# Weight remainders by engine, and two float64 weight chunks brought into the attention: a fused attention, expert and dense kernel

## The chip, the core and the metric

The kernel runs as one program on one core of a Trainium2 chip. The metric is the device time of one execution in microseconds (us), from the first to the last instruction with what the launch adds around it. The core has five instruction queues that matter here: PE (TensorE, matmuls), DVE (VectorE), ACT (ScalarE), POOL (GpSimd) and SP (SyncE, which here only issues DMAs). Each engine works its own queue strictly in order; semaphores tie the queues together.

## The reference

```python
scores = scale * q @ k.T                       # 2 batches, 8 heads, 768 positions, 64 wide
scores = where(is_sink | in_window, scores, -1e9)   # 4 sinks, window of 128
x = softmax(scores) @ v                        # 1536 tokens x 512

logits = x @ w_gate                            # 8 experts, capacity 192 each
order = argsort(-logits.flatten())             # greedy assignment, best pair first
for e in range(8):
    out[mask_e] = maximum(x[mask_e] @ w1[e], 0) @ w2[e]     # 512 -> 1024 -> 512

h = out @ w_in                                 # float64 weights, 512 -> 2048
y = (h * sigmoid(h)) @ w_out                   # float64 weights, 2048 -> 512
```

w1 and w2 come as float32; w_in and w_out come as float64 and reach the chip as pairs of 32-bit words.

## The kernel before

The program has four stages. **Attention** (`attention_band`, about 0 to 109 us) walks 96 heads (12 query blocks of 8 heads, index `n`), as a software pipeline written out by hand: in round `n` TensorE computes the scores of heads `n` and `n+1` (even `n`, `s_mm`), VectorE merges the two key blocks (`s_merge`, L261) and takes the row maximum (`s_max`, L268), ScalarE takes the exponential, TensorE transposes the head `n-5` and multiplies the head `n-13` with the values (`pv`). GpSimd cuts the transposed weights to the band (L299, L302). A dictionary `hooks` runs extra steps in given rounds. Every eight rounds SP gets the loads of a later block (keys three blocks ahead, values two), and TensorE computes the gate's products of one block (`vw`, L370). Scores, gate products and sink products share four PSUM buffers named `s`. **Routing** (to about 138 us) finds the assignment by iterations that go back and forth between VectorE and TensorE. **Experts** (`experts`, 145.5 to 310.4 us) and **dense** (`dense`, 310.4 us to the end) are TensorE loops over weights.

`Weights` feeds these two loops. The weights are 40 chunks of 128 x 2048: 32 of the experts (`k` = 0 to 31, float32), then 8 dense ones (`k` = 32 to 39, float64, "wide"). Each chunk is used as a high part and a remainder, in two halves: `hi` is a ScalarE copy of a half to fp32r (L884), and `lo` is the subtraction raw minus high (L888). A wide half must first be unpacked from 64-bit words into float32 by ten VectorE steps, five for each of its two quarters (`s0` to `s4`, L846 to L862). Raw pieces come through seven buffers `raw`: the step that uses one up issues the next load on SP. Four chunks `wr` are held at a time; `done(k)` lets chunk `k+4` begin. The steps `hi` and `lo` of a coming chunk stand in a list `todo`, those of unpacking in `back`; `pump(items, ops)` is called at fixed places of the TensorE loops (in `evac` after each half chunk of the experts, after each group of `dense`) and takes `items` of the first and `ops` of the second, so it decides where these steps stand in the queues of ScalarE, VectorE and GpSimd. Per expert `e` the TensorE order is `m1(e+1,0)`, `m2(e,0)`, `m1(e+1,1)`, `m2(e,1)`, one chunk each. After each half chunk `evac` takes the result out of PSUM by a ScalarE copy (L1010), a VectorE addition (L1011), a ScalarE step (L1013) and a VectorE subtraction (L1015 or L1017). GpSimd also gathers the experts' rows of `x` by indirect DMA (L956), three at a time.

Before the change a remainder runs on GpSimd, with one exception: while the experts run, every eighth half (`LO_DVE`) runs on VectorE. All sixteen wide remainders run on GpSimd. The unpacking of chunk 32 begins in the last two experts (`W.ahead(4 * E)` and the `ops` of 2 and 3 that `m1`, `m2` and `evac` hand on), with 5 steps per group in the first two groups of `dense`.

## Time and profile before

| | |
|---|---|
| median of 3 runs | 590.63 us (589.99 to 618.26) |
| the profiled execution | 593.17 us |
| its span, first to last instruction | 591.5 us |
| TensorE busy | 552.3 us (93%) |
| VectorE busy | 345.0 us (58%) |
| ScalarE busy | 254.2 us (43%) |
| GpSimd busy | 240.1 us (41%) |
| mean granted TensorE clock | 0.957 |

The shares are averages over four stages with different limits, so they say little by themselves. The views that help are the page's slices (one digit for each 14.8 us), the waits of TensorE, and the instructions in order of time around each wait. Matmuls are pipelined: what counts is the distance from one start to the next, not the length of one.

### The profile page before, as it was taken

What the parts mean: (1) busy time and instruction counts of PE and PEld (TensorE: products, weight loads), DVE (VectorE), ACT (ScalarE), POOL (GpSimd) and SP (SyncE); (2) the same over time, 40 slices, a digit from 0 to 9 for tenths busy, and PEclk for the clock granted to TensorE, in tenths of its full rate; (3) what the DMA queues carried; (4) which work ended last, traced back from release to release, by engine and by line L of the source; (5) the groups of instructions that cost most, each with busy time, mean ns of one, the idle gap of its engine ahead of it and who ended that gap; (6) DMA issues with size and microseconds to landing.
All of it is one profiled execution on the core that took longest, in us unless ns stands there. A gap on an engine that the chain in (4) does not pass through costs nothing.

```text
span 591.5 us, 9262 instructions
## 1 busy us (share of the span) xinstructions
PE 552.3 (93%) x3367; PEld 493.1 (83%) x3369; DVE 345.0 (58%) x852; ACT 254.2 (43%) x488; POOL 240.1 (41%) x212
## 2 busy tenths in 40 slices
PE   8999999547999999899987999999999999999996
PEld 4788788425899898899986888899889988999884
DVE  3665867871356658554787988659436963131312
ACT  4544544451575773776434334362223332222220
POOL 3333333376489799889831331122101230000124
PEclk9999999756999999799988999999999999999999
DMA  7846554053366566666642343233101000000022
GB/s 207 294 144 227 178 187 174 37 213 118 101 214 230 198 235 228 214 217 242 213 147 93 121 142 109 70 107 104 40 1 35 1 1 0 2 0 1 18 90 106
DMA packets 26367, 74.86 MB, mean 127 GB/s; under 512 B 3338, under 2 KB 4874, under 8 KB 26316
## 3 DMA queue, kind: packets, MB, share of 16 engines
q1 hardware_dynamic: 24128, 67.85, 34.0%
q0 software_dynamic: 1920, 6.29, 3.0%
q8 instruction: 29, 0.48, 0.3%
q14 instruction: 22, 0.18, 0.1%
q10 hardware_dynamic: 268, 0.06, 0.0%
HBM read 67.90 MB, written 6.29 MB: 125 GB/s over the span
## 4 chain that ended last, share of the span: by engine, by line
PE 53%; issue 8%; DVE 6%; POOL 4%; ACT 4%; DMA 1%; POOLq 0%; ACTq 0%; DVEq 0%
PE h L1111 7%; PE h L1112 6%; PE h L1113 6%; PE acc L1141 6%; PE acc L1142 6%; PE acc L1140 6%; PE mm L1030 6%; PE m L1053 4%; PE mm L1033 2%; POOL wr L888 2%; POOL out L1124 2%; PE m L1056 2%; ACT wr L884 2%; DVE f L858 1%; PE mm L993 1%
## 5 line engine op out<-in xcount | busy, mean ns | idle before, releaser
L888 POOL TENSOR_TENSOR wr<-raw,wr 128x1024 fp32r<-128x1024 f32 x57 | 136.9, 2434 | 28.9 <-ACT wr L884 28.7
L1117 DVE TENSOR_TENSOR gt<-sg,gt 128x384 fp32r<-128x384 f32 x64 | 52.1, 815 | 110.1 <-ACT gt L1116 108.6
L888 POOL TENSOR_TENSOR wr<-f,wr 128x1024 fp32r<-128x1024 f32 x16 | 39.2, 2452 | 145.4 <-ACT wr L884 77.9
L1111 PE MATMUL h<-x,wr 128*128 128x384 f32 x256 | 87.4, 341 | 4.6 <-ACT sg L1115 4.6
L1115 ACT ACTIVATE sg<-h 128x384 f32<-128x384 f32 x64 | 31.3, 489 | 140.4 <-PE h L1113 133.9
L1112 PE MATMUL h<-x,wr 128*128 128x384 f32 x256 | 86.8, 339 | 0.0
L1113 PE MATMUL h<-x,wr 128*128 128x384 f32 x256 | 86.6, 338 | 0.0
L1030 PE MATMUL mm<-xg,wr 128*128 128x384 f32 x256 | 78.4, 374 | 5.8 <-DVE ht L1015 5.8
L1141 PE MATMUL acc<-wr,gt 128*128 128x512 f32 x192 | 76.0, 396 | 0.0
L1142 PE MATMUL acc<-wr,gt 128*128 128x512 f32 x192 | 76.0, 396 | 0.0
L1140 PE MATMUL acc<-wr,gt 128*128 128x512 f32 x192 | 75.9, 395 | 0.0
L884 ACT ACTIVATE wr<-raw 128x1024 fp32r<-128x1024 f32 x64 | 66.9, 1058 | 4.2 <-DVE r L773 4.2
L1033 PE MATMUL mm<-xg,wr 128*128 128x192 f32 x256 | 65.7, 257 | 0.0
L1053 PE MATMUL m<-ht,wr 128*128 128x384 f32 x224 | 65.6, 361 | 0.0
L1056 PE MATMUL m<-ht,wr 128*128 128x192 f32 x224 | 56.1, 250 | 0.0
L1030 PEld LDWEIGHTS mm<-xg,wr 128*128 128x128 f32 x256 | 50.4, 197 | 6.8 <-DVE ht L1015 5.7
L1111 PEld LDWEIGHTS h<-x,wr 128*128 128x128 f32 x256 | 48.5, 190 | 7.6 <-ACT sg L1115 6.3
L1033 PEld LDWEIGHTS mm<-xg,wr 128*128 128x128 f32 x256 | 51.2, 200 | 0.1
L277 ACT ACTIVATE A<-t,nm 128x132 f32<-128x132 f32 x96 | 35.9, 399 | 32.5 <-DVE nm L268 32.5
L1112 PEld LDWEIGHTS h<-x,wr 128*128 128x128 f32 x256 | 48.6, 190 | 1.4
L1113 PEld LDWEIGHTS h<-x,wr 128*128 128x128 f32 x256 | 48.7, 190 | 0.0
L1124 POOL DMA_INDIRECT out<-osum,idx x12 | 11.8, 980 | 90.5 <-DVE osum L1148 89.4
(156 smaller groups left out, 1047.3 us busy)
## 6 DMA issues: line engine op xcount, KB each, us to landing
raw<-in_w SPq DMA_DIRECT2D x64, 512.0 KB, 3.1
raw<-in_wi SPq DMA_DIRECT2D x16, 512.0 KB, 3.9
raw<-in_wo SPq DMA_DIRECT2D x16, 512.0 KB
va<-in_va SPq DMA_DIRECT2D x12, 292.0 KB, 3.7
vt<-in_vt SPq DMA_DIRECT2D x12, 256.0 KB, 4.7
x_d<-x SPq DMA_DIRECT2D x12, 256.0 KB, 2.1
kall<-in_kd SPq DMA_DIRECT2D x10, 264.0 KB, 4.0
qr<-in_qd SPq DMA_DIRECT2D x10, 256.0 KB, 6.2
```

The source lines that it names most:

```text
L884: nc.scalar.activation(w[:, 0, sl], src(), AF.Copy)
L888: (self.lo or (nc.vector if dve else nc.gpsimd)).tensor_tensor(w[:, 1, sl], src(), w[:, 0, sl].bitcast(F32), OP.subtract)
L1030: nc.tensor.matmul(mm[:, b, :2 * CAP], w[:, 0, fb, d, o:o + P], x[:, d].rearrange("p a t -> p (a t)"), start=d == 0, stop=False, skip_grou ...
L1033: nc.tensor.matmul(mm[:, b, :CAP], w[:, 1, fb, d, o:o + P], x[:, d, 0], start=False, stop=d == 3, skip_group_check=True)
L1053: nc.tensor.matmul(mm[:, d % 2, :2 * CAP], w[:, 0, d // 2, f, o:o + P], ht[:, f].rearrange("p a t -> p (a t)"), start=c == 0 and f == 0, s ...
L1056: nc.tensor.matmul(mm[:, d % 2, :CAP], w[:, 1, d // 2, f, o:o + P], ht[:, f, 0], start=False, stop=last, skip_group_check=True)
L1111: nc.tensor.matmul(hv, w[:, 0, d, o:o + P], x2[:, d, 0, sx], start=d == 0, stop=False)
L1112: nc.tensor.matmul(hv, w[:, 0, d, o:o + P], x2[:, d, 1, sx], start=False, stop=False)
L1113: nc.tensor.matmul(hv, w[:, 1, d, o:o + P], x2[:, d, 0, sx], start=False, stop=d == 3)
L1140: nc.tensor.matmul(a, gt[:, 0, ts], w[:, 0, f], start=f == 0, stop=False)
L1141: nc.tensor.matmul(a, gt[:, 0, ts], w[:, 1, f], start=False, stop=False)
L1142: nc.tensor.matmul(a, gt[:, 1, ts], w[:, 0, f], start=False, stop=f == 3)
```

## The change

1. **Who subtracts.** `LO_DVE` goes: all 64 remainders of the expert chunks run on GpSimd, and those of the first two dense chunks (`early`, 32 and 33). Those of the six later dense chunks (`late`, 34 to 39) run on VectorE.
2. **Two wide chunks first.** The eight raw pieces of chunks 32 and 33 come before all others. The first seven loads are issued in the rounds 18, 20, ... 30 of the attention (before: seven loads of expert weights in round 84). Their 40 unpacking steps run one each in the rounds 27, 29, ... 93 and 38, 48, ... 88; every fifth one issues the next raw load on SP. Their results stay in the four buffers `f64` until the dense stage.
3. **Nothing is unpacked in the experts.** `W.ahead(4 * E)` and the `ops` handed on there go; in `dense` the first group pumps nothing and the others two steps.
4. **Silu's table.** A Silu of one column stands on ScalarE ahead of the experts.
5. **First gate products.** `vw(0)` moves from round 8 to 10, `sinks(0)` from 10 to 12.

```diff
-            if n in (VL + 2, NB * H + VL - 3):
+            if n in (VL + 2, NB * H + VL - 5):
+                vw(n // (NB * H) * NB)
+            if n in (VL + 4, NB * H + VL - 3):
                 sinks(n // (NB * H))
...
-LO_DVE = (5,)
+FIRST, EVEN, ODD = 18, (38, 48, 58, 68, 78, 88), range(27, 95, 2)
...
+        wide = [k for k, o in enumerate(order) if len(o) > 2]
+        self.early, self.late = wide[:2], wide[2:]
+        ks = self.early + [k for k in range(len(order)) if k not in self.early]
+        self.pieces = deque((k, src) for k in ks for src in order[k])
...
-                dve = not wide and (2 * k + half) % 8 in LO_DVE
-                (self.lo or (nc.vector if dve else nc.gpsimd)).tensor_tensor(
+                (nc.vector if k in self.late else nc.gpsimd).tensor_tensor(
...
-        if e == E - 2:
-            W.ahead(4 * E)
...
-        m2(e, 0, partial(hook, part=0), *((2,) if e >= E - 2 else ()))
+        m2(e, 0, partial(hook, part=0))
...
-            W.pump(1, 5 if (c, g, f) < (0, 0, 2) else UPB)
+            W.pump(1, UPB if (c, g, f) > (0, 0, 0) else 0)
...
-                hooks = {NT * H // 2: [load_route], NT * H - 12: [W.fetch]}
+                hooks = {NT * H // 2: [load_route]}
+                for k in range(W.raws):
+                    hooks.setdefault(FIRST + 2 * k, []).append(W.load)
+                for n in sorted({*EVEN, *ODD}):
+                    hooks.setdefault(n, []).append(W.unpacked)
...
-        W.started()
+        silu = cp.tile([P, 1], F32, name="silu")
+        nc.scalar.activation(silu, ident[:, 0:1], AF.Silu)
```

What this does to the queues, at three places. The first is VectorE in the attention, rounds 26 to 28. Before the change (L261 merges two scores, each pair L268 takes one maximum, L353, L354 and L358 finish an output):

```order
L261 COPY_PREDICATED s<-later,s 128x128 x2
L358 TENSOR_TENSOR lw<-X,rv 128x32
L268 ISA t,nm<-s,mask 128x132
L268 ISA nm 128x1
L268 ISA t,nm<-s,mask 128x132
L268 ISA nm 128x1
L261 COPY_PREDICATED s<-later,s 128x128 x2
```

The same place with the change (L850 and L854 are the unpacking steps `s0` and `s1`, at L846 and L850 before):

```order
L261 COPY_PREDICATED s<-later,s 128x128 x2
L358 TENSOR_TENSOR lw<-X,rv 128x32
L268 ISA t,nm<-s,mask 128x132
L268 ISA nm 128x1
L850 TENSOR_SCALAR f_540<-raw 128x512
L268 ISA t,nm<-s,mask 128x132
L268 ISA nm 128x1
L261 COPY_PREDICATED s<-later,s 128x128 x2
L268 ISA t,nm<-s,mask 128x132
L268 ISA nm 128x1
L854 TENSOR_SCALAR f_540<-f_540 128x512
```

In odd rounds an unpacking step now stands ahead of the maximum of the pair's second head, or ahead of L353. The second place is VectorE in the last experts, from the middle of chunk 28 into chunk 29, before the change (L1011, L1015 and L1017 belong to `evac`, the others are unpacking steps):

```order
L1015 SCALAR_TENSOR_TENSOR ht<-mm,ht 128x2x192
L862 SCALAR_TENSOR_TENSOR f_4229<-raw,f_4229 128x512
L846 TENSOR_SCALAR f_4229<-raw 128x512
L850 TENSOR_SCALAR f_4229<-f_4229 128x512
L1011 TENSOR_TENSOR mm<-mm,t 128x2x192
L1015 SCALAR_TENSOR_TENSOR ht<-mm,ht 128x2x192
L854 TENSOR_SCALAR f_4229<-f_4229 128x512
L858 SCALAR_TENSOR_TENSOR f_4229<-raw,f_4229 128x512
L862 SCALAR_TENSOR_TENSOR f_4229<-raw,f_4229 128x512
L1011 TENSOR_TENSOR m_4207<-m_4207,t 128x2x192
L1017 TENSOR_TENSOR x_2715<-m_4207,x_2715 128x2x192
```

The same place with the change (the three lines of `evac` are L1016, L1020 and L1022 there):

```order
L1020 SCALAR_TENSOR_TENSOR ht<-mm,ht 128x2x192
L1016 TENSOR_TENSOR mm<-mm,t 128x2x192
L1020 SCALAR_TENSOR_TENSOR ht<-mm,ht 128x2x192
L1016 TENSOR_TENSOR m_4272<-m_4272,t 128x2x192
L1022 TENSOR_TENSOR x_2780<-m_4272,x_2780 128x2x192
```

Between two evacuations nothing is left there. The third place is GpSimd from the start of the experts, before the change (the row gathers are L956; `wr<-raw` is a remainder of an expert chunk, `wr<-f` one of a dense chunk, and twelve more of these follow):

```order
L956 DMA row<-x_d,idx 128x512 x3
L888 TENSOR_TENSOR wr<-raw,wr 128x1024 x8
L956 DMA row<-x_d,idx 128x512 x3
L888 TENSOR_TENSOR wr<-raw,wr 128x1024 x14
L956 DMA row<-x_d,idx 128x512 x3
L888 TENSOR_TENSOR wr<-raw,wr 128x1024 x27
L888 TENSOR_TENSOR wr<-f_4229,wr 128x1024
L888 TENSOR_TENSOR wr<-f_4342,wr 128x1024
L888 TENSOR_TENSOR wr<-f_4487,wr 128x1024
L888 TENSOR_TENSOR wr<-f_4538,wr 128x1024
```

And with the change:

```order
L961 DMA row<-x_d,idx 128x512 x3
L891 TENSOR_TENSOR wr<-raw,wr 128x1024 x9
L961 DMA row<-x_d,idx 128x512 x3
L891 TENSOR_TENSOR wr<-raw,wr 128x1024 x16
L961 DMA row<-x_d,idx 128x512 x3
L891 TENSOR_TENSOR wr<-raw,wr 128x1024 x31
L891 TENSOR_TENSOR wr<-f_540,wr 128x1024
L891 TENSOR_TENSOR wr<-f_842,wr 128x1024
L891 TENSOR_TENSOR wr<-f_1110,wr 128x1024
L891 TENSOR_TENSOR wr<-f_1387,wr 128x1024
```

GpSimd has 56 expert remainders here instead of 49, and four dense ones instead of sixteen.

## Rows read from the trace of the kernel before

**Rows 1.** The page's slices, 40 equal ones: busy tenths.
```profile
PE   8999999547999999899987999999999999999996
...
DVE  3665867871356658554787988659436963131312
```

**Rows 2.** Waits of TensorE, whole run: us in total, times, longest us.
```profile
PE mm L1030 <- DVE ht L1015: 5.8, 4, 3.3
PE h L1111 <- ACT sg L1115: 4.6, 2, 4.1
...
PE mm L1053 <- DVE ht L1015: 2.4, 1, 2.4
...
PE s L370 <- DVE s L261: 0.3, 1, 0.3
```

**Rows 3.** Timeline of VectorE, then GpSimd, in the experts: start us, us, what.
```profile
169.63 1.23 DVE L888 TENSOR_TENSOR wr<-raw,wr 128x1024 fp32r<-128x1024 f32 x1 [0.58 <-ACT wr L884]
...
186.16 9.56 DVE L888 TENSOR_TENSOR wr<-raw,wr 128x1024 fp32r<-128x1024 f32 x1 [1.39 <-ACT wr L884]
...
182.82 11.80 POOL L888 TENSOR_TENSOR wr<-raw,wr 128x1024 fp32r<-128x1024 f32 x5
```

**Rows 4.** Timeline of TensorE in experts and dense: start us, us, what.
```profile
157.90 0.44 PE L1030 MATMUL mm<-xg,wr 128*128 128x384 f32 x1 [0.28 <-DVE ht L1015]
...
287.97 0.36 PE L1030 MATMUL mm<-xg,wr 128*128 128x384 f32 x1
...
292.52 0.36 PE L1053 MATMUL m<-ht,wr 128*128 128x384 f32 x1
...
310.44 0.36 PE L1111 MATMUL h<-x,wr 128*128 128x384 f32 x1
...
329.71 0.39 PE L1140 MATMUL acc<-wr,gt 128*128 128x512 f32 x1
...
333.91 0.33 PE L1111 MATMUL h<-x,wr 128*128 128x384 f32 x1
...
338.20 0.39 PE L1140 MATMUL acc<-wr,gt 128*128 128x512 f32 x1
```

**Rows 5.** TensorE's transposes of two gathered row tiles, in the chain of waits.
```profile
165.06 0.87 PE mm L993 x8
```

**Rows 6.** Groups by line and shape: count, busy us, mean ns; whole run, then 330 to 340 us.
```profile
L888 POOL TENSOR_TENSOR wr<-raw,wr 128x1024 fp32r<-128x1024 f32 x57 | 136.9, 2434 | 28.9 <-ACT wr L884 28.7
...
L862 DVE SCALAR_TENSOR_TENSOR f<-raw,f 128x512 int32<-128x512 int32 x3 | 2.1, 692 | 0.1
L850 DVE TENSOR_SCALAR f<-f 128x512 f32<-128x512 f32 x2 | 0.9, 428 | 0.1
```

**Rows 7.** GpSimd's timeline as the experts begin.
```profile
156.95 4.75 POOL L888 TENSOR_TENSOR wr<-raw,wr 128x1024 fp32r<-128x1024 f32 x2 [7.98 <-ACT wr L884]
...
180.60 0.95 POOL L956 DMA_INDIRECT row<-x_d,idx  x1 [0.30 <-issue]
```

**Rows 8.** ScalarE's timeline, end of routing and start of dense.
```profile
141.38 0.60 ACT L1003 ACTIVATE xg<-mm 128x512 fp32r<-128x512 f32 x1 [8.18 <-PE mm L993]
...
317.11 1.28 ACT L1115 ACT_TABLE_LOAD   x1
```

**Rows 9.** Windows: busy us of PE, PEld, DVE, ACT, POOL; granted clock; DMA share, GB/s.
```profile
20.00:25.00 5.00, 5.00 (x40) 3.74 (x40) 3.94 (x25) 2.57 (x7) 2.15 (x6) 1.00 1.02 380
28.00:98.00 70.00, 70.00 (x546) 56.42 (x545) 45.35 (x263) 32.60 (x90) 24.29 (x57) 1.00 0.58 196
58.00:68.00 10.00, 10.00 (x78) 7.70 (x77) 8.15 (x44) 4.51 (x12) 3.08 (x7) 1.00 0.48 164
```

**Rows 10.** Timelines in the attention: VectorE's two L379, GpSimd beside the second.
```profile
14.76 0.76 DVE L379 TENSOR_TENSOR vsr<-vsf,vsr 32x584 fp32r<-32x584 f32 x1
...
61.80 1.14 DVE L379 TENSOR_TENSOR vsr<-vsf,vsr 32x584 fp32r<-32x584 f32 x1
...
61.69 0.64 POOL L299 TENSOR_SCALAR_AFFINE_SELECT atd<-at 128x512 f32<-128x512 f32 x1 [2.87 <-ACT at L297]
```

More of the change, by code (lines that the diff above doesn't have):

```diff
@@ L428, in attention_band @@
             it, ht = divmod(n - VL, H)
-            if ht == 0 and 0 <= it < NT and it != NB:
+            if ht == 0 and 0 < it < NT and it != NB:
                 vw(it)
-            if n == NB * H + VL - 5:
-                vw(NB)
-            if n in (VL + 2, NB * H + VL - 3):
+            if n in (VL + 2, NB * H + VL - 5):
+                vw(n // (NB * H) * NB)
+            if n in (VL + 4, NB * H + VL - 3):
                 sinks(n // (NB * H))
@@ L805, with __init__ @@
 UPB, DNB = 2, 1
-LO_DVE = (5,)
+FIRST, EVEN, ODD = 18, (38, 48, 58, 68, 78, 88), range(27, 95, 2)
 class Weights:
-    def __init__(self, tc, pool, order, depth, raws, scratch):
-        self.nc = tc.nc
+    def __init__(self, tc, pool, f64, order, depth, raws, scratch):
+        self.nc, self.f64 = tc.nc, f64
         self.rawp, self.order, self.depth, self.raws, self.scratch = pool, order, depth, raws, scratch
-        self.pieces = deque((k, src) for k, o in enumerate(order) for src in o)
+        wide = [k for k, o in enumerate(order) if len(o) > 2]
+        self.early, self.late = wide[:2], wide[2:]
+        ks = self.early + [k for k in range(len(order)) if k not in self.early]
+        self.pieces = deque((k, src) for k in ks for src in order[k])
         self.raw = {k: deque() for k in range(len(order))}
@@ L816, in __init__ @@
         self.ns = 0
-        self.lo = None
+        for k in self.early:
+            self.ahead(k)
     def load(self):
@@ L844, in s0 @@
                 if part == 0:
-                    box.append(self.pool.tile([P, CH // 2], I32, name="f64", bufs=self.scratch))
+                    box.append(self.f64.tile([P, CH // 2], I32, name="f64", bufs=self.scratch))
                 nc.vector.tensor_scalar(box[0][:, sl], word(1), 0x7FFFFFFF, None, OP.bitwise_and)
@@ L894, in split, with unpack_all @@
             self.todo += [(0, hi, (k, half)), (0, lo, (k, half))]
+    def unpack_all(self):
+        while self.back:
+            self.unpacked()
     def unpacked(self):
+        if not self.back:
+            return
         f, key = self.back.popleft()
@@ L924, in start @@
             self.split()
-        self.lo = self.nc.gpsimd
     def preload(self, n, items=99):
@@ L930, in preload @@
             items -= 1
-    def started(self):
-        self.lo = None
     def get(self, k, halves=(0, 1)):
@@ L1080, in hook @@
                     gather(m + 1)
-        if e == E - 2:
-            W.ahead(4 * E)
         if e + 1 < E:
             m1(e + 1, 0)
-        m2(e, 0, partial(hook, part=0), *((2,) if e >= E - 2 else ()))
+        m2(e, 0, partial(hook, part=0))
         if e + 1 < E:
-            m1(e + 1, 1, ops=3 if e == E - 2 else 0)
-        m2(e, 1, partial(hook, part=1), 3 if e == E - 2 else 0)
+            m1(e + 1, 1)
+        m2(e, 1, partial(hook, part=1))
 def dense(tc, wp, pp, idx, W, nxt, x2, out):
@@ L1205, in fused @@
         raws = ctx.enter_context(tc.tile_pool(name="raws", bufs=1, reuse_waits="tile"))
-        W = Weights(tc, raws, order, 4, 7, 4)
+        f64 = ctx.enter_context(tc.tile_pool(name="f64s", bufs=1, reuse_waits="tile"))
+        W = Weights(tc, raws, f64, order, 4, 7, 4)
         rest = ExitStack()
@@ L1217, in fused @@
                                ident, x_d, L, pp, hooks)
+                W.unpack_all()
                 route.values(L, NT - 1, NT)
@@ L1221, in fused @@
                 W.fetch()
+                W.unpack_all()
                 attention(tc, *(a[k] for k in ("qd", "kd", "vd", "wg")), n_sink, window, ident, x_d, L)
```

## The prediction

> **What bounds the kernel now.** I read the page's slices first. TensorE is busy in nine tenths or more of nearly every slice; it falls off around 105 to 140 us (routing) and, less, where experts and dense meet, near 300 to 330 us [rows 1]. So TensorE's work bounds all stages but routing, and a change can only win where TensorE waits or give back where it makes it wait. The waits of TensorE name the first kind: four waits in the experts, 5.8 us, for VectorE's step L1015 of the evacuation; one of 2.4 us in the last chunk but one; and 4.6 us at the start of dense for Silu's output, which there waits behind VectorE [rows 2]. After 330 us TensorE waits for nothing, so whatever brings the dense stage forward by 1 us ends the kernel 1 us earlier.
>
> Then the timelines around these waits. At 186.16 us VectorE begins a remainder that takes 1.23 us elsewhere, and it lasts 9.56 us: it ends 1.1 us after a run of five remainders on GpSimd (182.82 + 11.80 = 194.62 us) has ended [rows 3]. VectorE's evacuation stands behind it, so TensorE waits. Seen from the row, an operation of VectorE on two SBUF operands is held until GpSimd falls idle.
>
> The Trainium skill, "SBUF — State Buffer", section "Who interferes with whom", says that VectorE and GpSimd share one pair of ports under an exclusive lock, for one whole instruction. By that the hold would be at most one remainder of 2.36 us; this row shows 9.56 us, through four ends of an instruction, and so the row decides.
>
> **The change, part by part.** *Experts.* TensorE's own pace is one chunk per 4.55 us (287.97 to 292.52) [rows 4]. Chunk 2 starts at 157.90; the 30 chunks from there are 136.5 us, and three pairs of experts add their transposes, 0.87 us for two row tiles [rows 5] and half that for the third, 1.3 us each, 3.9 us in all. TensorE alone would reach dense at 157.9 + 140.4 = 298.3 us; it did at 310.44 [rows 4]. The 12.1 us between are the stalls and what they entail. The change removes all SBUF-only work of VectorE from this stage: the seven remainders and the unpacking.
>
> It puts seven more remainders on GpSimd. That is the price: 56 remainders at 11.80/5 = 2.36 us [rows 3] are 132.2 us, six gathers at 0.95 + 0.30 us [rows 7] 7.5 us. From 156.95 us [rows 7], with about 1 us of waiting while the first chunks arrive (an estimate from the same timeline), GpSimd is done at 297.7 us; the last half remainder feeds half a chunk, 2.28 us. So dense starts at 300.0 us, not 298.3: GpSimd becomes the bound of the last experts by 1.7 us. Gain: 310.4 − 300.0 = **10.4 us**. Bounds: 12.1 us if GpSimd keeps ahead; if a remainder costs the mean of the whole run, 2.434 us [rows 6], 56 × 0.074 = 4.1 us less, 6.3 us.
>
> *Start of dense.* Three groups go ahead of the first `down`. A group takes 338.20 − 333.91 = 4.29 us, three 12.9 us; before they took 329.71 − 310.44 = 19.3 us [rows 4]. The stall there is Silu's table, 1.28 us [rows 8], and the unpacking of chunks 32 and 33 ahead of VectorE's part of the output. Both are gone: **6.4 us**. Bounds: 1.3 us (the table alone, if VectorE is as late with chunk 34) and 6.4. I take the upper, since the order shows three subtractions of the output ahead of the first unpacking step. GpSimd's remainders of chunks 32 and 33 end at 300.1, 302.4, 304.8 and 307.2 us by its pace; dense needs them at 300, 308.6 and 312.9 us. The table costs nothing in its new place, since ScalarE there waits 8.18 us for gathered rows [rows 8]; without that cover it costs 1.3 us.
>
> The Trainium skill, "ScalarE: Activation LUTs", section "What ACT_TABLE_LOAD costs", gives 1283 ns for the load and 1380 ns of draining, 2.66 us a switch; the row has the same load, and by the page this term would be 2.66 us instead of 1.3 us, inside the 6.4 us either way.
>
> *Later dense.* Twelve remainders move to VectorE at 1.23 us [rows 3], 14.8 us over 256 us in which TensorE never waited and VectorE's slices stand between one and nine tenths [rows 1]. The subtraction that TensorE needs is made two groups ahead, so nothing is charged; GpSimd no longer holds the unpacking up there. If that cover were gone, the twelve would cost at most 14.8 us.
>
> *Attention.* This is where the change pays. Forty steps come to VectorE, eight pieces of three at 0.43 and two at 0.69 us [rows 6], 2.67 us each, 21.4 us. From 28 to 98 us VectorE is busy 45.35 of 70 us while TensorE is busy all 70 [rows 9]. Together 66.7 us: it just fits, if no step waits for GpSimd. GpSimd is busy 24.29 us there, 35%. One row shows such a meeting: L379 takes 1.14 us beside a band cut of 0.64 us, and 0.76 us alone [rows 10]. If a step that meets a cut waits half of it, 0.32 us, the forty wait 40 × 0.35 × 0.32 = 4.5 us and VectorE needs 71.2 us, 1.2 us too many. If it waits for the whole run of cuts and casts, about 2 us long, half of that is 1 us, the waits are 14 us, and VectorE needs 80.7 us, 10.7 us too many. Besides, from 58 to 68 us VectorE is at 8.15 of 10 us [rows 9] and gets six steps, 3.2 us: 1.35 us over. Two engines near full with only four score buffers between them lose something more. I charge **4 us**: 1.2 + 1.35 and 1.5 for that friction (an estimate), nearer to the low end because most steps fall into gaps in which the cuts are done. Bounds: 0 and 12 us.
>
> The port rule of the Trainium skill named above speaks against this edit, since band cuts read SBUF as the steps do; by one instruction at a time it gives the 1.2 us case, and the first L379 row pair agrees with it.
>
> *DMA and queues.* Seven pieces of 512 KB go out between rounds 18 and 30, when the DMA engines are full (share 1.02, 380 GB/s, at 20 to 25 us) [rows 9]. At that rate they take 9.7 us. On SP they stand behind the loads of block 5 and ahead of those of block 6, which are needed 16 rounds or more later, about 17 us at 1.06 us a round: hidden; if not, up to 9.7 us. The eight later loads make SP wait for an unpacking step, with output writes and block loads behind it; those have the same 17 us.
>
> *First gate products.* Worth the wait at L370, **0.3 us** [rows 2], at most; nothing at least.
>
> **Sum**, against the profiled execution's span of 591.5 us: −10.4 − 6.4 − 0.3 + 4.0 = −13.1, 578.4 us. That execution took 593.2 us, 2.6 us above the median of 590.6 us, so I carry the difference over: 590.6 − 13.1 = **577.5 us**.
>
> **The rivals.** *A. The attention is bound by VectorE*: every step waits out GpSimd's whole run. For it: the 9.56 us row. Against it: in the experts GpSimd's instructions follow each other without a gap, here they come in short groups. Charge 12 instead of 4: 585.5 us. *B. GpSimd limits the experts more*, at 2.434 us a remainder: 581.6 us. Against it: that mean contains the meetings with VectorE which are removed. *C. The dense start keeps its stall* with chunk 34 in place of 32, only the table is won: 582.6 us. *D. Slower*: the steps stand directly ahead of a row maximum, and scores, maximum and transposes are one chain; if TensorE waited for every step and its port wait, 21.4 + 14 = 35.4 us would land on the path: 590.6 − 17.1 + 35.4 = 608.9 us. It decides from 28.9 us on (82% of the inserted time), for then the time is 2% above 590.6. Against it: VectorE now waits for scores, not TensorE for VectorE (TensorE has no idle time at all from 28 to 98 us). *E. It does not do what it says*: the experts' stalls come from something else, and 6.4 us of dense and 4 us of attention are all there is: 588 us. Against it: the ends in rows 3 match within 1.1 us.
>
> **How the numbers follow.** Forecast 0.58, A 0.18, B 0.10, C 0.06, D 0.04, E 0.04. The forecast's own range is 572 (attention free, GpSimd ahead: 590.6 − 12.1 − 6.4 − 0.3 = 571.8) to 581. The range for 8 in 10 takes in A, B and C: 572 to 586. Faster by over 2% means below 578.8 us, about what a measurement can tell from no change: most of the forecast, 0.53, and the good edge of A and B, 0.02, together 0.55; slower, over 602.4 us, is D, 0.04; within 2% the rest, 0.41.
>
> **What would show it.** In the changed profile: TensorE's waits for the evacuation gone from the experts; no VectorE row with an SBUF-only step between 145 and 300 us; GpSimd's remainders without gaps from about 215 us on, TensorE waiting for them by a few tenths per chunk near the end; the first `down` 13 us after the first `up`; no table load there; in the attention VectorE busy over nine tenths, last scores 2 to 6 us later. I am wrong if the attention ends more than 8 us later, or if TensorE waits for GpSimd by more than 4 us in the experts.

## The result and the profile after

The kernel after takes **575.8 us** (median of four executions, 574.8 to 576.9) against 591.05 us (four of before): ratio 0.975, 95% interval 0.972 to 0.978. It is faster by about 15 us, where 577.5 was predicted. The ratio leaves out one execution of before that took 618.3 us; of 38 later ones ten took 670 to 673 us at a granted clock of 0.83, while none of the 23 of after and of the experiments with its attention took over 584.4 us, and no profile tells why. The profiled execution of after took 575.27 us, with a span of 573.6 us against 591.5.

The slices, which answer to [rows 1], and the granted clock:

```profile
PE   9999999727999999999999999999999999999996
...
DVE  3787898973334443443338774665438843141312
...
PEclk9999999856999999999999999999999999999999
```

VectorE is fuller in slices 2 to 7 (the attention, 14 to 100 us) but for the fifth, which is level, and emptier in the experts; TensorE's dent where experts and dense meet is gone. The waits of TensorE over the whole run (us in total, times, longest) answer to [rows 2]; the routing's 12.3 us at L631 are the same before:

```profile
PE s L631 <- DVE G L618: 12.3, 6, 3.1
PE mm L998 <- DMA row<-x_d,idx: 2.3, 2, 2.1
...
PE mm L1035 <- DVE ht L1020: 1.1, 2, 0.8
PE s L255 <- DVE nm L268: 0.4, 1, 0.4
```

Of the four waits for the evacuation, 5.8 us, two are left, together 1.1 us, both before 157 us in the first chunks. The wait of 2.4 us in the last chunk but one, the 4.6 us for Silu and the 0.3 us at L370 are gone. From 157 to 560 us the list has no wait of TensorE, and its clock is 1.00.

Where the 17.9 us between the two spans lie is read from four events on TensorE's timeline: the first product of the second half of expert 0 (L1058, L1053 before), the first `up` (L1114), the first `down` (L1143) and the end.

| | before | after | difference of the stretch |
|---|---|---|---|
| first L1058 (L1053) | 162.58 | 161.34 | −1.2 |
| first `up` | 310.44 | 298.15 | experts 147.86 → 136.81, −11.1 |
| first `down` | 329.71 | 310.82 | 19.27 → 12.67, −6.6 |
| span | 591.5 | 573.6 | rest 261.8 → 262.8, +1.0 |

```profile
161.34 0.36 PE L1058 MATMUL m<-ht,wr 128*128 128x384 f32 x1
...
298.15 0.36 PE L1114 MATMUL h<-x,wr 128*128 128x384 f32 x1
...
310.82 0.40 PE L1143 MATMUL acc<-wr,gt 128*128 128x512 f32 x1
```

The first row of the table is no gain: in nine profiled executions this event lies between 161.3 and 164.2 us, by when the gathered rows land and when TensorE's clock has risen again after routing (first pairs of products at a spacing of 0.29 us in after, 0.53 us for five pairs before). The medians differ by 15.2 us and not by 17.9 for that reason, and because the profiled execution of before was one of its longer ones.

### The profile page after: what moved, and what is told of

It is laid out like the page before. It is cut to its first block, busy times and chain, and to the rows that moved or that the text cites. A ratio compares the mean times of both kernels' runs of the same rounds, so it can differ in the third digit from the quotient of the medians.

```text
span 573.6 us, 9225 instructions
## 1 busy us (share of the span) xinstructions
PE 547.8 (96%) x3369; PEld 489.1 (85%) x3369; DVE 302.4 (53%) x857; ACT 257.4 (45%) x489; POOL 226.2 (39%) x207
## 4 chain that ended last, share of the span: by engine, by line
PE 68%; issue 3%; POOL 2%; ACT 1%; DMA 1%; DVE 0%; POOLq 0%; ACTq 0%
PE mm L1035 8%; PE m L1058 8%; PE h L1116 7%; PE h L1114 7%; PE h L1115 7%; PE acc L1144 7%; PE acc L1145 7%; PE acc L1143 7%; PE mm L1038 4%; PE m L1061 4%; POOL out L1127 2%; PE mm L1058 1%; PE mm L998 1%; DMA row<-x_d,idx 1%; PE mm L1061 1%
## 5 line engine op out<-in xcount | busy, mean ns | idle before, releaser
L891 POOL TENSOR_TENSOR wr<-raw,wr 128x1024 fp32r<-128x1024 f32 x64 | 150.7, 2386 | 10.3 <-ACT wr L888 10.2
L1120 DVE TENSOR_TENSOR gt<-sg,gt 128x384 fp32r<-128x384 f32 x64 | 39.3, 615 | 123.2 <-ACT gt L1119 121.1
L1114 PE MATMUL h<-x,wr 128*128 128x384 f32 x256 | 86.5, 338 | 0.0
L1143 PE MATMUL acc<-wr,gt 128*128 128x512 f32 x192 | 75.9, 395 | 0.0
L1035 PE MATMUL mm<-xg,wr 128*128 128x384 f32 x256 | 74.7, 360 | 1.1 <-DVE ht L1020 1.1
L888 ACT ACTIVATE wr<-raw 128x1024 fp32r<-128x1024 f32 x64 | 66.7, 1052 | 7.3 <-DVE r L773 4.2
L1058 PE MATMUL m<-ht,wr 128*128 128x384 f32 x224 | 66.0, 361 | 0.0
L1038 PE MATMUL mm<-xg,wr 128*128 128x192 f32 x256 | 64.3, 251 | 0.0
L1035 PEld LDWEIGHTS mm<-xg,wr 128*128 128x128 f32 x256 | 48.2, 188 | 1.7 <-PE mm L1038 1.0
L1038 PEld LDWEIGHTS mm<-xg,wr 128*128 128x128 f32 x256 | 49.0, 191 | 0.3
L1115 PEld LDWEIGHTS h<-x,wr 128*128 128x128 f32 x256 | 48.0, 188 | 1.4
L1114 PEld LDWEIGHTS h<-x,wr 128*128 128x128 f32 x256 | 48.1, 188 | 1.3
L1116 PEld LDWEIGHTS h<-x,wr 128*128 128x128 f32 x256 | 48.1, 188 | 0.0
L1145 PEld LDWEIGHTS acc<-wr,gt 128*128 128x128 f32 x192 | 36.1, 188 | 8.7
```

The costliest lines, as they stand in the source:

```text
L888: nc.scalar.activation(w[:, 0, sl], src(), AF.Copy)
L891: (nc.vector if k in self.late else nc.gpsimd).tensor_tensor(w[:, 1, sl], src(), w[:, 0, sl].bitcast(F32), OP.subtract)
L1035: nc.tensor.matmul(mm[:, b, :2 * CAP], w[:, 0, fb, d, o:o + P], x[:, d].rearrange("p a t -> p (a t)"), start=d == 0, stop=False, skip_grou ...
L1038: nc.tensor.matmul(mm[:, b, :CAP], w[:, 1, fb, d, o:o + P], x[:, d, 0], start=False, stop=d == 3, skip_group_check=True)
L1058: nc.tensor.matmul(mm[:, d % 2, :2 * CAP], w[:, 0, d // 2, f, o:o + P], ht[:, f].rearrange("p a t -> p (a t)"), start=c == 0 and f == 0, s ...
L1114: nc.tensor.matmul(hv, w[:, 0, d, o:o + P], x2[:, d, 0, sx], start=d == 0, stop=False)
```

## The experiments

All are the kernel after with one edit, unless said otherwise.

### One expert remainder in eight back on VectorE

```diff
-(nc.vector if k in self.late else nc.gpsimd).tensor_tensor(
+(nc.vector if k in self.late or (3 < k < 32 and (2 * k + half) % 8 == 5) else nc.gpsimd).tensor_tensor(
```

> The kernel after, but seven of the 56 half-chunk remainders of the experts (one in eight, from chunk 6 on) are back on VectorE; the unpacking in the attention, the table and the later dense part stay as in the kernel after. Theory (VectorE's remainders are held for as long as GpSimd works without a pause, and the evacuation stands behind them): rows of 8 to 11 us on VectorE in the experts, waits of TensorE for the evacuation of 5 to 6 us come back, and with what they entail the time rises by 6 to 12 us, to 582 to 588. Rival (GpSimd is the bound of the experts by its 2.36 us a remainder, so relieving it of seven pays): the time stays within 2 us of 575.8 or falls.

582.25 us, 6.4 above after; the experts take 143.56 us instead of 136.81. Waits of TensorE, then VectorE's and GpSimd's timelines:

```profile
PE mm L1035 <- DVE ht L1020: 5.8, 4, 3.2
...
187.19 9.56 DVE L891 TENSOR_TENSOR wr<-raw,wr 128x1024 fp32r<-128x1024 f32 x1 [1.39 <-ACT wr L888]
...
183.87 11.80 POOL L891 TENSOR_TENSOR wr<-raw,wr 128x1024 fp32r<-128x1024 f32 x5
```

The picture of [rows 3] to the hundredth: GpSimd's run ends at 195.67, VectorE's remainder at 196.75. The rival (relieving GpSimd pays) is out: these seven remainders are worth 6.7 us of the 11.1.

Only two of the seven are held like this, the one shown and one of 11.35 us. The other five take 1.2 to 1.8 us, and three of them begin in the middle of a run of GpSimd. One of these three:

```profile
210.76 1.31 DVE L891 TENSOR_TENSOR wr<-raw,wr 128x1024 fp32r<-128x1024 f32 x1 [0.58 <-ACT wr L888]
...
199.15 22.26 POOL L891 TENSOR_TENSOR wr<-raw,wr 128x1024 fp32r<-128x1024 f32 x9 [3.49 <-ACT wr L888]
```

VectorE is done here at 212.07, while GpSimd goes on without a pause to 221.41; its run of nine takes 1.0 us more than nine of 2.36. So VectorE can also be let in between two instructions of GpSimd. The theory, as it was put, is too strong: GpSimd's run can hold VectorE to its end, but it need not.

### The unpacking back where it was

```diff
-self.early, self.late = wide[:2], wide[2:]
+self.early, self.late = [], wide[2:]
...
+        if e == E - 2:
+            W.ahead(4 * E)
...
-W.pump(1, UPB if (c, g, f) > (0, 0, 0) else 0)
+W.pump(1, 5 if (c, g, f) < (0, 0, 2) else UPB)
```

> The kernel after, but chunks 32 and 33 are loaded and unpacked where the kernel before did it (the last two experts and the first groups of dense), and nothing is unpacked in the attention; the remainders stay on GpSimd in the experts and on VectorE later, the table stays ahead. Theory (the move pays at the start of dense and costs nothing to speak of in the attention): the first down comes 17 to 18 us after the first up instead of 12.7, waits of TensorE in the last experts of about 2.4 us return, and the time rises by 5 to 8 us, to 581 to 584. Rival 1 (the attention pays about 4 us for its 40 steps, as I had forecast): the rise is only 1 to 4 us, and the last scores come about 4 us earlier than in the kernel after. Rival 2 (the stall at the start of dense was the table alone): the time stays within 1 us of 575.8.

594.43 us: **18.6 above after, and above the kernel before** (ratio 1.006, 1.002 to 1.009). None of the three expectations was near. The start of dense gives what was expected, 18.48 us from first `up` to first `down` instead of 12.67, but the experts take 149.76 us instead of 136.81. The wait of TensorE; VectorE's and GpSimd's timelines; the windows (columns as in [rows 9]):

```profile
PE mm L1058 <- DVE ht L1020: 8.6, 2, 8.1
...
285.86 7.96 DVE L850 TENSOR_SCALAR f<-raw 128x512 int32<-128x512 int32 x1 [8.35 <-DMA raw<-in_wi]
293.85 0.43 DVE L854 TENSOR_SCALAR f<-f 128x512 f32<-128x512 f32 x1
...
279.53 13.99 POOL L891 TENSOR_TENSOR wr<-raw,wr 128x1024 fp32r<-128x1024 f32 x6
...
285.00:290.00 5.00, 4.00 (x28) 3.71 (x26) 4.14 (x1) 0.00 (x0) 5.00 (x3) 1.00 0.63 197
290.00:295.00 5.00, 0.00 (x0) 0.00 (x0) 4.90 (x4) 0.00 (x0) 3.52 (x2) 0.82 0.78 245
295.00:300.00 5.00, 2.89 (x11) 2.89 (x12) 4.41 (x6) 1.82 (x3) 2.13 (x1) 0.50 0.49 139
```

With all expert remainders on GpSimd, GpSimd works without a pause to 293.52, and a single unpacking step, 0.42 us elsewhere, is held for 7.96 us until 0.3 us after that. (VectorE had stood 8.35 us for that step's DMA before; TensorE worked until 289.0 us in spite of it, and of the time from there to its next product, at 297.11 us, the hold is 7.5 us, 7.96 less 0.42.) TensorE stands for 8.1 us, and then its granted clock is at the lower level, 0.50, from 295 to 305 us; so the stall costs a second time. The two halves of the change are thus not a sum. The unpacking move without the remainders' move (the experiment ahead of this one) gains about 9 us on the kernel before, the remainders' move without the unpacking's loses about 3, both together gain 15. (Both kernels also have the small parts of the change, which below are worth nothing that these runs can tell.) Each removes a part of VectorE's SBUF-only work from the stage in which GpSimd has no pauses, and the remainders' move is what takes the pauses away: without it GpSimd makes its remainders in runs of 5 to 9 from 183 to 292 us, in after in runs of 16 and 31.

By the Trainium skill, "SBUF — State Buffer", section "Who interferes with whom", the hold lasts for one whole instruction, here 2.33 us. The row shows 7.96 us, so the measurement decides, as in [rows 3]; the remainder of 1.31 us in the run before this one agrees with the page.

### A wait put into GpSimd's run

The kernel of 582.25 us, with a small copy on GpSimd out of what VectorE wrote:

```diff
+                if dve:
+                    nc.gpsimd.tensor_copy(self.dum, w[:, 1, sl][:, :8].bitcast(F32))
```

> The kernel with seven remainders of the experts on VectorE (582.25 us), where GpSimd now also makes a small copy out of each of these seven before its next remainder, so that it waits until VectorE has written and is idle meanwhile. Theory (VectorE's instruction is held as long as GpSimd goes from instruction to instruction without a pause, and let in when it pauses): the seven rows of VectorE fall from 9.5 us to at most 3.6 (1.23 and what is left of one remainder), TensorE's 5.8 us of waiting for the evacuation are gone, and the time is that of the kernel after or a little less, 574 to 578. Rival (VectorE's remainder is late for another reason, or GpSimd loses as much by waiting as it is spared): 580 to 584.

577.75 us, 4.5 less than without the copy, and the experts are down from 143.56 to 136.68 us, the level of after. TensorE's wait for the evacuation, and the two timelines:

```profile
PE mm L1038 <- DVE ht L1023: 1.8, 3, 0.8
...
187.75 7.24 DVE L892 TENSOR_TENSOR wr<-raw,wr 128x1024 fp32r<-128x1024 f32 x1 [1.39 <-ACT wr L888]
...
184.47 9.45 POOL L892 TENSOR_TENSOR wr<-raw,wr 128x1024 fp32r<-128x1024 f32 x4
195.06 0.19 POOL L895 COPY dum<-wr 128x8 f32<-128x8 f32 x1 [1.15 <-DVE wr L892]
```

VectorE is let in when GpSimd pauses, at 193.92, and is done 1.07 us later. So a pause of GpSimd ends the hold, as the theory says. My 3.6 us a row was wrong for the two long rows (7.24 and 8.74 us), since GpSimd was behind by remainders that stood ahead of the copy in its own order; the run became one remainder shorter (four instead of five), and that was enough for TensorE. The other five rows take 1.2 to 3.3 us; four of them were let in at the end of one GpSimd remainder, without a pause. Over the kernel before, the run with seven remainders on VectorE and this one, 15 remainders of VectorE began while GpSimd had at least one more to make without a pause: six were held to the end of that run, nine were let in at the next end of a remainder. What decides between the two stays open.

### More work for GpSimd

```diff
+                if not wide and k > 3:
+                    nc.gpsimd.memset(self.dum, 0.0)
```

> The kernel after with a small fill of a 128x64 tile on GpSimd behind each half-chunk remainder of the experts from chunk 4 on (56 of them), by an estimate from the 0.09 us fill of one element 0.1 to 0.2 us each, 6 to 11 us in all. Theory of the prediction (GpSimd is the bound of the last experts, its last remainder ends just as the first matmul of dense starts): TensorE waits for GpSimd near the end and the time rises by nearly all of it, 5 to 10 us. Rival (GpSimd ends with time in hand, up to four chunks ahead): nothing, or only what exceeds its lead, 0 to 3 us.

581.31 us; the experts take 141.12 us, 4.3 more, of 56 × 0.084 = 4.7 us that the fills add: from one remainder to the next GpSimd takes 2.44 us over the last 31 (227.10 to 302.74 us), where it takes 2.356 in after. GpSimd's timeline, then TensorE's:

```profile
292.99 2.38 POOL L891 TENSOR_TENSOR wr<-raw,wr 128x1024 fp32r<-128x1024 f32 x1
295.32 0.14 POOL L894 MEMSET dum<- 128x64 f32 x1
295.42 2.39 POOL L891 TENSOR_TENSOR wr<-raw,wr 128x1024 fp32r<-128x1024 f32 x1
...
292.99 0.36 PE L1063 MATMUL m<-ht,wr 128*128 128x192 f32 x1
...
295.42 0.36 PE L1063 MATMUL mm<-ht,wr 128*128 128x192 f32 x1
```

TensorE's first product of a remainder starts when GpSimd has ended that remainder and goes on to the next, half-chunk by half-chunk. The list of waits shows 1.1 us of this at most, because TensorE's rows are modelled as touching. So nearly all of what the fills add came through to the end: GpSimd is the bound of the last experts. After's own rows show the same in small. Its last 31 remainders take 2.356 us each, where TensorE alone needs 4.55/2 = 2.28 us for a half-chunk, and TensorE's first product of each remainder lasts 0.30 to 0.33 us instead of 0.25:

```profile
222.88 73.04 POOL L891 TENSOR_TENSOR wr<-raw,wr 128x1024 fp32r<-128x1024 f32 x31
...
288.67 0.25 PE L1061 MATMUL m<-ht,wr 128*128 128x192 f32 x1
288.96 0.30 PE L1061 MATMUL mm<-ht,wr 128*128 128x192 f32 x1
...
291.28 0.33 PE L1061 MATMUL mm<-ht,wr 128*128 128x192 f32 x1
...
293.64 0.32 PE L1061 MATMUL mm<-ht,wr 128*128 128x192 f32 x1
```

### Small parts: the table, the later dense part, the gate products

```diff
-        silu = cp.tile([P, 1], F32, name="silu")
-        nc.scalar.activation(silu, ident[:, 0:1], AF.Silu)
```

> The kernel after without the early Silu, so that its table is loaded at the first Silu of dense. Theory (1.28 us on the path, before the first down): 1.3 us more, 577.1, the first down 13.9 us after the first up instead of 12.65. Rival 1 (ScalarE is ahead by more than that, two groups of up work being in flight): no change, 575.8. Rival 2 (a switch costs 2.66 us, by the Trainium skill, page ScalarE: Activation LUTs, section What ACT_TABLE_LOAD costs): 578.5.

576.37 us, no difference; first `up` to first `down` 12.52 us. The load lies in the first group, where ScalarE is ahead:

```profile
301.62 1.28 ACT L1118 ACT_TABLE_LOAD   x1
302.91 0.49 ACT L1118 ACTIVATE sg<-h 128x384 f32<-128x384 f32 x1
```

So in this kernel the table costs nothing. In the kernel before it did stand in the way: there the load ends at 318.39 us ([rows 8]), 0.02 us ahead of the first Silu, for whose output TensorE was waiting. The kernel with the unpacking back and the table ahead takes 18.48 us for this stretch, before 19.27; so up to 0.8 of the 6.6 us may be the table's (one execution of each). The Trainium skill, "ScalarE: Activation LUTs", section "What ACT_TABLE_LOAD costs", adds 1380 ns of draining to the load; here Silu starts 0.01 us behind the load's end, and the row decides.

```diff
-(nc.vector if k in self.late else nc.gpsimd).tensor_tensor(
+nc.gpsimd.tensor_tensor(
```

> The kernel after with the remainders of the later dense chunks (34 on) on GpSimd again, twelve of 2.36 us. Theory (those of chunks 34 and 35 come when nothing waits for VectorE closely, TensorE never waits in the later dense): the unpacking steps beside them take up to 2 us longer, and the time stays within 0.6 us of 575.8. Rival (an unpacking step held by GpSimd's remainder holds the subtraction of the output that TensorE needs two groups later): TensorE waits for VectorE in dense and the time rises by 1 to 5 us.

576.54 us, no difference. VectorE does meet GpSimd there (the unpacking step below is held until GpSimd's remainder ends at 322.88), but TensorE does not wait:

```profile
320.45 2.43 POOL L891 TENSOR_TENSOR wr<-f,wr 128x1024 fp32r<-128x1024 f32 x1 [14.11 <-ACT wr L888]
...
320.53 2.63 DVE L850 TENSOR_SCALAR f<-raw 128x512 int32<-128x512 int32 x1
```

The gate products and sinks two rounds earlier again, as in the kernel before:

> The kernel after with the first gate products and the sinks at the rounds of the kernel before (8 and 10 instead of 10 and 12). Theory (they are worth the wait of 0.3 us in the trace of before and no more): TensorE waits 0.3 us at L370 again and the time stays within 0.6 us of 575.8. Rival (with VectorE this full in the attention the order there matters, and a gap early in the stage lets the clock fall): 2 us or more.

577.82 us (576.4, 576.9, 578.8 and 585.8; ratio to before 0.976, 0.971 to 0.981, which overlaps after's). In the profile TensorE does not wait at L370; it waits 0.8 us for VectorE at the scores (L255) instead of 0.4, and GpSimd's first gather starts at 138.67 us instead of 137.72. A difference of about 1 us is possible, none is shown; the execution of 585.8 us has no profile.

### How much more fits into the attention

An idle step of VectorE (a 128x512 shift on its own tile, 0.43 us) behind each of the forty unpacking steps, then two behind each:

```diff
         f()
+        if self.dum is not None:
+            for _ in range(1):
+                self.nc.vector.tensor_scalar(self.dum, self.dum, 3, 0x3FFFFFFF, OP.logical_shift_left, OP.bitwise_and)
```

> The kernel after with one more step of VectorE behind each of the forty unpacking steps of the attention (an idle shift on a 128x512 tile of its own, 0.43 us). The forty real steps raised VectorE's busy time from 28 to 98 us by 13.7 us (45.35 to 59.09) and moved the gather of the experts' rows by only 0.8 us. Theory (the attention has room until VectorE's busy time fills the 70 us, and then pays the excess): about 11 us more, 70 of 70 us, so 1 to 3 us on the total, 577 to 579. Rival 1 (each step lands on the path between scores and maximum): 16 us more, 592. Rival 2 (steps wait for GpSimd's cuts once VectorE is this full): 4 to 8 us more.

> The kernel after with two more such steps behind each of the forty, 34 us of VectorE's work more. Theory: VectorE's sum is now about 81 us for the 70 us of the stage, so it is the bound and the attention ends about 11 us later: 587. Rival 1 (all of it on the path): 34 us more, 610. Rival 2 (nothing, VectorE's work still fits because rows overlap): 576 to 578.

613.48 and 636.22 us, 37.7 and 60.4 above after: about twice what even the rival that puts every step on the path gives. Windows of the first of the two:

```profile
38.00:48.00 10.00, 10.00 (x72) 7.61 (x73) 10.00 (x43) 4.28 (x12) 3.65 (x7) 1.00 0.72 243
...
53.00:54.00 1.00, 1.00 (x10) 1.00 (x11) 1.00 (x5) 0.76 (x3) 0.60 (x1) 1.00 0.63 70
54.00:55.00 1.00, 1.00 (x10) 0.91 (x8) 1.00 (x4) 0.40 (x1) 0.93 (x2) 0.84 0.63 205
55.00:56.00 1.00, 1.00 (x8) 0.78 (x5) 1.00 (x5) 0.00 (x0) 1.00 (x4) 0.50 0.97 383
...
58.00:68.00 10.00, 10.00 (x45) 7.98 (x45) 3.99 (x21) 2.27 (x7) 1.27 (x2) 0.50 0.70 238
```

VectorE is full, 10 of 10 us; TensorE's matmuls, which wait for it, become fewer (72 in 10 us, where after has 81); and at 54.7 us TensorE's granted clock drops from 1.00 to 0.50. From then on TensorE is the slow one, VectorE falls to 4 of 10 us, and the attention goes on at half speed (the clock is back from about 89 to 102 us and then falls again). To see whether the clock is the cost, the same forty idle steps with more matmuls (each second score product made twice, the second over the first):

```diff
-nc.tensor.matmul(s[:, :j - b0 + 1], Q[i][d, h // 2], kall[d, b0:j + 1, h // 2], start=True, stop=True)
+for _ in range(1 + o):
+    nc.tensor.matmul(s[:, :j - b0 + 1], Q[i][d, h // 2], kall[d, b0:j + 1, h // 2], start=True, stop=True)
```

> The kernel of 613.48 us (one idle step behind each of the forty unpacking steps), in which TensorE makes every second score product twice, the second time over the first: 48 matmuls more, about 0.16 us each at the full clock, 7.7 us. Theory (VectorE's fullness alone costs little; TensorE's matmuls come more thinly while it is held up by VectorE, 67 to 72 per 10 us instead of 75 to 84, and the clock falls for that): with more matmuls in the same time the clock stays at 1.00 for most or all of the attention and the time falls in spite of the added work, to 578 to 600. Rival (the clock falls for another reason, or VectorE's own work is what costs): 611 to 622.

600.10 us, 13.4 us less with more work. The whole stage keeps its clock:

```profile
78.00:88.00 10.00, 9.81 (x62) 7.52 (x63) 9.64 (x46) 4.62 (x12) 2.64 (x7) 1.00 0.55 188
...
28.00:98.00 70.00, 69.58 (x501) 56.41 (x499) 60.65 (x274) 27.48 (x74) 22.50 (x46) 1.00 0.67 228
```

So the clock is a large part of the price: 13.4 us came back net, and if the 48 added matmuls cost their time (7.7 us), 21 of the 37.7. The rest is not told apart; the 24.3 us that this kernel is above after are about the sum of what was added (40 × 0.43 + 7.7 = 24.9 us). How near is the edge? Twenty idle steps behind every second unpacking step, and then twenty again, with none between rounds 38 and 73:

> The kernel after with one idle step of 0.43 us behind every second unpacking step of the attention: 20 steps, 8.6 us, where 40 such steps (16 us) cost 37.7 us because TensorE's granted clock fell to 0.50 from 54.8 us on, after VectorE had been full for ten us. Theory A (what costs is the clock, and it falls once VectorE is full for a while; from 58 to 68 us the kernel after already stands at 9.51 of 10 us): VectorE's busy time from 28 to 98 us rises by about 7 us to 66, the clock falls in some stretch, and the time rises by far more than 8.6 us, by 10 to 30: 586 to 606. Theory B (there is room for about this much): the clock stays at 1.00 and the time rises by 0 to 2 us: 576 to 578. Rival (each step lands on the path): 8.6 us more, 584.5.

> Again 20 idle steps of 0.43 us on VectorE in the attention, but all of them behind the unpacking steps up to round 38 and from round 73 on; none in between, where (about 41 to 77 us, with the sinks of the second sequence at 61 us) the clock fell when they stood behind every second step (613.4 us in two executions, 581.2 in a third). Theory (what decides is one stretch that VectorE fills, not its sum): VectorE's busy time over the stage is as large as there, the clock stays at 1.00 from 28 to 98 us, and the time is 576 to 580 in nearly every execution. Rival (the sum decides, or any full stretch will do): the clock falls in most executions, around 613 us or, falling later, 595 to 605.

The executions of one kernel differ here by their clock, so they are given one by one: 613.4, 613.3 and 581.2 us (granted clock over the run 0.905, 0.904, 0.970) for the first; 630.9, 630.9, 630.7, 630.7, 598.7 and 580.8 us for the second. With 8.6 us of work more, the clock sometimes holds, and then it costs 5 us, and in seven of nine executions it falls. (That it falls in the attention is read from the two profiled executions, one of each kernel; for the others only the clock over the run is known.) Of the 23 executions with this attention and nothing added none fell so, but the kernel before did in some, so these steps are not the only way to such a fall. Windows of the second, in the execution of 598.7 us:

```profile
58.00:68.00 10.00, 9.64 (x69) 7.15 (x68) 8.88 (x40) 4.10 (x10) 2.96 (x6) 1.00 0.55 193
68.00:78.00 10.00, 10.00 (x73) 7.79 (x73) 9.84 (x51) 5.46 (x15) 3.36 (x8) 1.00 0.62 219
78.00:88.00 10.00, 9.79 (x70) 7.70 (x70) 9.61 (x42) 4.52 (x14) 3.85 (x8) 0.96 0.42 139
88.00:98.00 10.00, 10.00 (x43) 7.71 (x42) 6.44 (x25) 2.59 (x7) 2.91 (x7) 0.50 0.10 32
```

My theory that the one stretch from 58 to 68 us decides fell: without a step there the clock fell in five of six executions, here at 87 us, behind two stretches in which VectorE was at 9.84 and 9.61. Nor does a full VectorE suffice: with the added matmuls it was at 9.64 from 78 to 88 us and the clock held. What exactly lets it fall in one execution and not in another stays open.

## Why the prediction was right, and where it was not

**Experts, −10.4 forecast: −11.1 measured** (147.86 to 136.81 us; 136.8 to 137.1 in the nine kernels with after's experts). What was forecast of this stage came: no SBUF-only row of VectorE in the experts, no evacuation stall after the first chunks, GpSimd without a gap from 181.55 us on but for its row gathers (the group below answers to [rows 6]: 2.386 us mean instead of 2.434), and GpSimd the bound of the end by a little, as the added fills showed. This bound was forecast to cost 1.7 us; dense starts at 298.15 where the forecast for TensorE alone, less the 1.2 us that the experts began earlier, is 297.1, so about 1 us. Of the 11.1 us the seven remainders are 6.7 (143.56 − 136.81) and the other 4.3 came with the rest of the change, of which only the unpacking touches this stage.

```profile
L891 POOL TENSOR_TENSOR wr<-raw,wr 128x1024 fp32r<-128x1024 f32 x64 | 150.7, 2386 | 10.3 <-ACT wr L888 10.2
```

What the stalls "entail" can be named: the waits that are gone are 7.1 us (5.8 − 1.1 + 2.4), and the rest fits the clock. In the kernel before, TensorE's granted clock is at the lower level for part of the time from 235 to 245 us, during and behind its stall of 3.3 us, and again from 300 to 310 us (0.71 and 0.95 in the two halves), behind the one of 2.4 us; by these shares that is at most 5 us lost, an estimate. In after it stays at 1.00 from 157 us on. Two windows of before, columns as in [rows 9]:

```profile
235.00:240.00 5.00, 1.73 (x7) 1.50 (x7) 3.77 (x5) 2.58 (x6) 1.50 (x2) 0.72 0.54 171
240.00:245.00 5.00, 5.00 (x23) 5.00 (x23) 2.84 (x6) 4.80 (x8) 5.00 (x3) 0.60 0.57 212
```

One reading behind this forecast was too strong. "Held until GpSimd falls idle" was read from one row of 9.56 us; of the seven remainders of VectorE in that same profile only two were held so (9.56 and 11.38 us), and two others, 1.30 and 1.38 us, were let in in the middle of a run of GpSimd:

```profile
209.75 1.30 DVE L888 TENSOR_TENSOR wr<-raw,wr 128x1024 fp32r<-128x1024 f32 x1 [0.58 <-ACT wr L884]
...
198.12 22.28 POOL L888 TENSOR_TENSOR wr<-raw,wr 128x1024 fp32r<-128x1024 f32 x9 [3.49 <-ACT wr L884]
```

The forecast did not suffer, since the change takes all seven away.

**Start of dense, −6.4 forecast: −6.6 measured**, 12.67 us to the first `down` where 12.9 was forecast. The split was wrong: the table was counted for 1.28 us of it. With the unpacking gone it costs nothing, since it falls into time in which ScalarE is ahead; with the table ahead and the unpacking back, the stage takes 18.48 us, so 5.8 us are the unpacking's, and the 0.8 us left are the most that the table can have cost beside it, if executions differ by less.

**Later dense, 0 forecast, 0 measured** for the remainders, by putting them back. The stretch from the first `down` to the end came out 1.0 us longer than before; in the kernel without the early table it is 573.2 − 312.24 = 261.0 us, 1.8 less than in after, and that edit touches nothing there. So a difference of this size is one between executions.

**First gate products, −0.3 at most:** the wait at L370 is gone; putting them back gave no difference in time that these runs can tell. The first gather, told below, points to more than the forecast: it starts 0.8 us earlier with the gate products moved, both without the unpacking in the attention (136.94 to 136.11) and, by 0.8 to 1.4 us, with it (138.67 against 137.3 to 137.9). These are mostly single executions, so it is not shown.

**Attention, +4 forecast: about +1 measured, and for the wrong reason.** GpSimd's first gather of rows, which follows the routing, starts at 137.72 instead of 136.94 us. Over the profiles it lies at 137.3 to 137.9 in six kernels with this attention, and at 136.1 and 136.9 in the two without the unpacking there. The nearest comparison, 136.1 with the gate products moved as in after, makes the unpacking's price 1.2 to 1.8 us. The windows answer to [rows 9]:

```profile
28.00:98.00 70.00, 69.64 (x533) 55.81 (x531) 59.09 (x295) 33.12 (x89) 25.59 (x54) 1.00 0.64 227
58.00:68.00 10.00, 9.64 (x67) 7.00 (x65) 9.51 (x45) 4.47 (x11) 2.49 (x5) 1.00 0.56 200
```

Two steps of the working failed. The sum 45.35 + 21.4 = 66.7 us was too high: the steps took what was forecast (39 of them 20.5 us in this window, 0.42 and 0.69 us each), but rows of VectorE overlap in time, so that durations add up to more than the busy time, and that rose by 13.7 us only (45.35 to 59.09); besides, a few of the attention's own rows moved out of the window (295 rows against 263, 32 more and not 39). So VectorE came to 84% where over nine tenths was forecast. And the waits for GpSimd's cuts, 1.2 to 10.7 us in the working, did not come: no step took over 0.69 us. In the attention GpSimd is busy 25.6 of 70 us, in short instructions with pauses; in the last experts it has none. The seven early loads cost nothing that the list of waits shows. Rivals A, B, C and E are out: the attention did not pay 12 us, a remainder takes 2.36 us, the dense start lost its stall, and the experts' stalls came back with the seven remainders. In rival D the place was right and the law was wrong: a slowdown in the attention does not grow with the time inserted up to 28.9 us; with 8.6 us more it sets in at once in seven of nine executions and costs 23 to 55 us, and TensorE's clock falls with it. My range did not hold that case, and the kernel after stays only that far from it.

By the terms the forecast was 3.9 us too high (attention 3.0, experts 0.7, start of dense 0.2), by the medians 1.7 (577.5 against 575.8). The other 2 us are of the size by which single executions differ (574.8 to 576.9 for after), and the terms were read from one execution of each kernel. That the total came within 2 us is in part luck, since the attention's term was off by 3 us and the two executions compared differ from the medians by nearly as much.

## What to carry to other kernels

Where GpSimd works without a pause, a VectorE instruction on SBUF operands alone can be held for the whole run (six of 15 remainders here, and an unpacking step), and everything behind it in VectorE's queue with it; look for a VectorE row that ends just behind a GpSimd run, count how many of its kind are held and how many not, and move all such work out of that stage, since moving half of it made it worse here. Work goes best to a stage in which GpSimd comes in short groups, but its room is not the idle time that the windows show: here, with VectorE near full, TensorE's clock fell, at a price far above the time inserted. A change that lands near this edge should be tried with a little work added, and in several executions.

## What the runs showed that was not expected

- TensorE counts as busy 10 of 10 us while it waits a little for VectorE between matmuls; the count of its matmuls in a window (81, then 72) shows it, and in that run the granted clock then fell from 1.00 to 0.50 at 54.7 us. The count alone foretells nothing: with 67 matmuls in 10 us (after, 58 to 68 us) and with 62 (the added matmuls, 78 to 88 us) the clock stayed at 1.00.
- The hold is not a matter of two SBUF operands: a VectorE step with one (L850) was held for 7.96 us.
- A stall of 8.1 us in the experts was followed by about 10 us at a clock of 0.50.
